# Retention into two expert layers: three tile shapes a pair in place of five, and raw weights asked for on a written schedule

## The chip, the cores and the metric

The kernel runs on one core of a Trainium2 chip. The metric is device time in microseconds (us), the median of three runs of the whole program.

## What is computed

```python
def _attn_ref(q, k, v):                       # B=4, H=8, S=576, D=64
    scores = scale * np.matmul(q, k.transpose(0, 1, 3, 2))
    gamma = 1.0 - 2.0 ** (-5.0 - np.arange(H, dtype=np.float32))
    Dmat = np.where(rel >= 0, gamma[:, None, None] ** rel[None, :, :], 0.0)
    return np.matmul(scores * Dmat[None, :, :, :], v)
def _moe_ref(x, w_gate, w_val, w_out):        # 2304 tokens, 512 wide, 1536 hidden
    g = x @ w_gate
    return (g * (1.0 / (1.0 + np.exp(-g))) * (x @ w_val)) @ w_out
def _moe2_ref(x, w_in, w_out):                # 512 wide, 2048 hidden
    r = np.maximum(x @ w_in, 0.0)
    return (r * r) @ w_out
```

A causal retention with one decay for each head, and behind it two dense layers on its output, called expert layers here. Their weights lie in DRAM as 64-bit words that hold a number's bits in another layout; the kernel turns them into 32-bit floats itself ("conversion").

## The kernel before

**Retention** works on 16 pairs of heads, four to a batch. A pair has its 576 positions in blocks of 128, the last one 64 wide. For pair `n` (loop in line 571) TensorE makes the scores inside each block (`scores`, line 453: two heads, 64 rows by 128 columns of the array each), DVE multiplies them by the mask into `p_sb`, or `pl` for the last block, and TensorE makes `sums` of k and v for each block (in `states`, line 472), from which ACT (a copy) and DVE (two steps) build the states `sb` that are carried from block to block. The outputs of a pair come later: `apply` (line 507) multiplies the carried states with the scaled queries `qs` (64 by 64 tiles) and then the masked scores with v (128 by 64), and ACT copies the result into `xy` (`put`). `old` is the pair whose outputs are made while pair `n` has its scores and sums: the one before for the first pairs, then two before (`LAG`). So TensorE's order in a pair is: scores, outputs of the old pair's four blocks, scores of the last block, output of the old pair's last block, sums.

**Buffers.** The scores of four blocks have two PSUM buffers, those of the last block one. The last output and the sums share a bank (`kv`). qk tiles and k tiles have three buffers, v five. One order is kept on each engine during retention: the `Chained` wrappers (line 100) issue each instruction behind the last one of its engine.

**Loads** are all issued by SP, in program order: the qk, k and v tiles of pair `n + 2` (576, 256 and 320 KB), then raw weights of 512 KB if there is a place (`prefetch`, line 130). There are two buffers in `raw_p` and one, `raw3`, that goes round in `spare`. The raw weight with index `n - LOADS_FROM` is allowed from pair `n` = 3 on; a load into a buffer that is still being converted holds SP until it is free, with all that stands behind it.

**Conversion** (`words`, line 158) takes two ACT and four DVE instructions a weight, given out in five units by `pump`: up to 25 units, five weights, during retention, from pair 5 on four a pair. DVE and ACT also build the first operands (`wi`, `wb`) and, from pairs 10 and 14 on, the differences of tokens (`xy`) and their split into a high and a low part (`xo_h`, `xo_l`, `xs`), one pair of tiles for each of seven operands (`renew`, line 297).

**Expert stages** follow: seven products of Strassen's kind for each system of weights, given out by slots (line 815), each of three matmuls for the high and low parts. Their order is no longer chained; the scheduler sets it.

Of the kernel before, what the change touches and what calls it, by code (L numbers as in the profile page):

```python
# [9 lines left out]
F32 = mybir.dt.float32  # L10
F32R = mybir.dt.float32r
U16 = mybir.dt.uint16
U32 = mybir.dt.uint32
AF = mybir.ActivationFunctionType
ALU = mybir.AluOpType
PSUM = bass.MemoryType.PSUM

B, H, S, D = 4, 8, 576, 64
# [3 lines left out]
P = 128  # L22
# [3 lines left out]
NC = -(-S // P)  # L26
N = 512
M0 = 256
M1 = 512
# [14 lines left out]
WARM = 5  # L44
UNITS_EARLY = 5
HOLD = 5
LOADS_FROM = 3

PACE = {(1, 0): (10, 1.6, 0.3), (1, 1): (8, 2.0, 0.0), (2, 0): (2, 0.0, 1.0)}

# [3 lines left out]
STATE = (0, 1, 3, 5)  # L54
# [7 lines left out]
def retention_moe_kernel(  # L62
# [13 lines left out]
    def pool(stack, name, bufs, **kw):  # L76
        return stack.enter_context(
            tc.tile_pool(name=name, bufs=bufs, reuse_waits="tile", **kw)
        )
# [10 lines left out]
    ps_g = pool(ctx, "ps_g", 1, space=PSUM)  # L90
# [33 lines left out]
    order = [(1, what, f) for k in range(F1 // 2) for what in "gvo" for f in (2 * k, 2 * k + 1)]  # L124
    order += [(2, what, f) for k in range(F2 // 2) for what in "io" for f in (2 * k, 2 * k + 1)]
    raw_t, w_t = {}, {}
    spare, ready = [], {}
    loads = {"next": 0, "raw": 0, "open": False, "cap": len(order) - 1, "held": 0, "turn": 0}

    def prefetch(upto):  # L130

        while loads["next"] <= min(upto, len(order) - 1):
            i = loads["next"]
            if loads["raw"] < 2:
                loads["raw"] += 1
                flat, back = raw_p.tile([P, 1024], U32, tag="raw", name="raw"), False
            elif spare:
                flat, back = spare.pop(0), True
            else:
                return  # L140
            loads["next"] += 1
            ph, what, f = order[i]
            src = (w1, w2)[ph - 1][f, :, ("gvo", "io")[ph - 1].index(what), :].bitcast(U32)
            sp.dma_start(out=flat.rearrange("p (a n) -> p a n", a=2), in_=src.rearrange("p (a n) -> p a n", a=2))
            raw_t[i] = flat, back
# [41 lines left out]
    def conversion():  # L187
        for i, key in enumerate(order):
            while loads["held"] > HOLD - 1:
                yield "held"  # L190
            prefetch(max(i, min(i + 4, loads["cap"])))
            flat, back = raw_t[i]
            for n, wt in enumerate(words(flat)):
                if n == 2:
                    finish(i - 1)
                else:
                    yield
            del raw_t[i]
            if not back:
                loads["raw"] -= 1  # L200
            elif loads["open"]:
                spare.append(flat)
            if key[0] == 1:
                ready[key] = wt.bitcast(F32)
                loads["held"] += 1
            else:
                w_t[i] = wt
            yield
        finish(len(order) - 1)
        yield  # L210
# [38 lines left out]
    def pump(k=1):  # L249
        for _ in range(k):  # L250
            if pumped["n"] < pumped["limit"]:
                pumped["n"] += next(convert, None) != "held"
# [127 lines left out]
    xo_p = pool(ctx, "xo_p", 1, side="right")  # L380

    with ExitStack() as st:
# [6 lines left out]
        sb_p = pool(st, "sb_p", 3)  # L389
        ps_s = pool(st, "ps_s", 1, space=PSUM)  # L390

        qk_t, k_t, v_t, q_t, p_t, sb_t = ({} for _ in range(6))
        rs = [slice(h * D, (h + 1) * D) for h in range(2)]
        pairs = [(b, hp) for b in range(B) for hp in range(NP)]
# [50 lines left out]
        def width(c):  # L445
            return min(P, S - c * P)
# [6 lines left out]
        def scores(n, cs):  # L453

            w, nx, hp = width(cs[0]), len(cs), pairs[n][1]
            ps = ps_s.tile([P, 2, 512], F32, tag=f"s{nx}", name="s", bufs=1 + (nx > 1))
            for x, c in enumerate(cs):
                at = slice(c * P, c * P + w)
                for h, r in enumerate(rs):
                    pe.matmul(  # L460
                        ps[:w, h, x * w:(x + 1) * w], qk_t[n][r, 1, at], qk_t[n][r, 0, at],
                        start=True, stop=True, skip_group_check=True,
                    )
            pt = p_p.tile([P, 2, nx, w], F32, tag="p", name="p_sb") if nx > 1 else p_last[n % 3]
            dve.tensor_tensor(
                out=pt[:w], in0=ps[:w, :, :nx * w].rearrange("p h (c q) -> p h c q", c=nx),
                in1=mask_sb[:w, hp, :, None, :w].to_broadcast([w, 2, nx, w]), op=ALU.mult,
            )
            for x, c in enumerate(cs):
                p_t[n, c] = pt[:, :, x, :]  # L470

        def states(new, old):


            bank = ps_g.tile([P, 512], F32, tag="v", name="kv")
            if old is not None:
                apply(old, True, bank[:, 256:256 + D])
            if new is None:
                put(old, True, bank[:, 256:256 + D])
                return  # L480
            kt, vt = k_t[new], v_t[new]
            ps = bank[:, :256].rearrange("p (c d) -> p c d", d=D)
            for c in range(NC - 1):
                for r in rs:
                    pe.matmul(
                        ps[r, c], kt[:, c, r], vt[:, c, r], start=True, stop=True,
                        skip_group_check=True,
                    )
            if old is not None:
                put(old, True, bank[:, 256:256 + D])  # L490
            sb_t[new] = sb = sb_p.tile([P, 6, D], F32, tag="sb", name="sb")
            hp = pairs[new][1]
            act.copy(sb[:, 0:6:2], ps[:, :3])
            for scalar, at, before, sums in (
                (qs_sb[:, hp, -1:], slice(1, 6, 2), sb[:, 0:6:2], ps[:, 1:]),
                (decay2[:, hp], slice(3, 6, 2), sb[:, :2], sb[:, 3:6:2]),
            ):
                dve.scalar_tensor_tensor(
                    out=sb[:, at], in0=before, scalar=scalar, in1=sums, op0=ALU.mult, op1=ALU.add,
                )  # L500

        def put(n, last, bank):
            b, hp = pairs[n]
            t0 = b * S + last * (NC - 1) * P
            act.copy(xy[:, hp, t0:t0 + bank.shape[-1]], bank)

        def apply(n, last, bank):

            cs = (NC - 1,) if last else range(NC - 1)

            def dst(c):
                return bank if last else bank[:, c * P:(c + 1) * P]

            for c in (cs if last else range(1, NC - 1)):
                at = slice((c - 1) * P, (c - 1) * P + width(c))
                for r in rs:
                    pe.matmul(
                        dst(c)[r], sb_t[n][r, STATE[c - 1]], q_t[n][r, at],
                        start=(c in (1, NC - 1)), stop=False, skip_group_check=True,
                    )  # L520
            for c in cs:
                pt = p_t.pop((n, c))
                for h, r in enumerate(rs):
                    pe.matmul(
                        dst(c)[r], v_t[n][:, c, r], pt[:, h, :],
                        start=False, stop=True, skip_group_check=True,
                    )

# [38 lines left out]
        last = len(pairs) - 1  # L567
        pumped["limit"] = 5 * UNITS_EARLY
        loads["open"] = True
        spare.append(raw2_p.tile([P, 1024], U32, tag="raw", name="raw3"))  # L570
        for n in range(last + 1 + LAG):
            new, nxt = n <= last, n + 1 <= last
            old = n - 1 if 1 <= n <= SOON else n - LAG if n > SOON + 1 else None
            if n + 2 <= last:
                load_qk(n + 2)
                load_kv(n + 2)
            if n >= LOADS_FROM:
                loads["cap"] = n - LOADS_FROM
                prefetch(loads["cap"])
            if new:  # L580
                scores(n, range(NC - 1))
            fill = int(n > LOADS_FROM + 1)
            pump(2 * fill)
            if old is not None:
                bank_o = ps_g.tile([P, 512], F32, tag="g", name="o")
                apply(old, False, bank_o)
                put(old, False, bank_o)
            if new:
                scores(n, (NC - 1,))
            if new or old is not None:  # L590
                states(n if new else None, old)
            if nxt:
                prep_state(n + 1)
            begin(n, 1)
            pump(fill)
            begin(n, 0)
            if n == 0:
                warm(1)
            pump(fill)
            if n % 2:  # L600
                begin(n, 1)
            else:
                catch_up()
# [180 lines left out]
    for n, (ph, p, k, what) in enumerate(systems):  # L784
        if what == "v":
            for x, which in enumerate("acb" if p == 0 else "ab"):
                at = n + 3 if which == "b" and n < flip - 1 else n + 2
# [27 lines left out]
    for n in range(end + 4):  # L815
        ph, p, k, what = systems[n] if n < end else (0, None, 0, "")
# [119 lines left out]
```

## Time and profile before

| | us |
|---|---|
| median of three runs | 875.05 (874.41 to 877.57) |
| profiled execution, span from the first to the last instruction | 875.1 |
| TensorE busy (PE) | 863.9, 99% |
| DVE busy | 642.8, 73% |
| ACT busy | 400.9, 46% |
| POOL busy | 122.2, 14% |

The profile is of one execution; its span and the median differ by less than 0.1 us. Matmuls overlap, so TensorE's busy time only says where it has nothing at all. "Releaser" is the instruction or transfer whose end let a waiting engine go on. A retention matmul in 32-bit floats stands as two instructions in the trace and as one in the program's order.

### The profile page before, as it was taken

The page shows a single profiled execution, that of the slowest core. Times are in us where ns is not written, and L with a number is a line of the kernel's source. Part 1 is how long each engine was busy: PE and PEld are TensorE (multiplying, and loading weights), DVE is VectorE, ACT ScalarE, POOL GpSimd, SP SyncE. Part 2 cuts the span into 40 slices and gives each one's busy share as a digit, 9 for nine tenths or more (in the row PEclk, how much of TensorE's full clock was granted, in tenths as well). Part 3 has the DMA queues.
Part 4 walks back from the last instruction along what each step waited for, and adds up shares of the span by engine and source line. Part 5 has one row for each costly group of instructions (what it writes and reads, how often), then busy time and mean ns, then how long its engine had stood idle before and what let it go on. Part 6 is the DMA issues. An engine that isn't in the chain of part 4 may idle for free.

```text
span 875.1 us, 13516 instructions
## 1 busy us (share of the span) xinstructions
PE 863.9 (99%) x5064; PEld 746.0 (85%) x5064; DVE 642.8 (73%) x1002; ACT 400.9 (46%) x709; POOL 122.2 (14%) x135
## 2 busy tenths in 40 slices
PE   9989999999999999999999999999999999999998
PEld 7878888888888888888888899989899988998987
DVE  3899999998976899677647999999534467533544
ACT  3657777565544544644325466554233233232310
POOL 3343343223130010000002311120000000000000
PEclk9999999999999999999999999999999999999999
DMA  9994777755554489878745388988666465656412
GB/s 337 402 356 160 253 249 249 264 186 211 196 192 154 139 282 379 297 273 288 253 141 185 144 315 328 361 304 313 206 239 215 126 226 210 190 202 204 164 41 73
DMA packets 75218, 203.62 MB, mean 233 GB/s; under 512 B 7696, under 2 KB 18448, under 8 KB 75152
## 3 DMA queue, kind: packets, MB, share of 16 engines
q1 hardware_dynamic: 74720, 202.34, 65.8%
q8 instruction: 40, 0.66, 0.3%
q10 hardware_dynamic: 432, 0.41, 0.1%
q14 instruction: 26, 0.21, 0.1%
HBM read 138.23 MB, written 64.49 MB: 232 GB/s over the span
## 4 chain that ended last, share of the span: by engine, by line
PE 86%; DVE 7%; DMA 4%; issue 2%; ACT 1%; SPq 0%; POOL 0%; DVEq 0%; POOLq 0%; ACTq 0%
PE oacc L113 42%; PE g L113 24%; PE v L113 12%; PE z L113 6%; DVE w L113 3%; DMA qk_sb<-in_qk 3%; DVE wi L113 1%; PE o L113 1%; DMA k_sb<-in_kv 1%; DMA qs_sb<-in_qscale 1%; PE s L113 1%; DVE xy L113 1%; DVE cbg L113 0%; PE kv L113 0%; DVE xo_l L113 0%
## 5 line engine op out<-in xcount | busy, mean ns | idle before, releaser
L113 PE MATMUL g<-xo_h,wi 128*128 128x384 f32 (+1 forms) x768 | 238.3, 364 | 0.0
L113 PE MATMUL oacc<-wo,ho_hi 128*128 128x512 f32 (+1 forms) x584 | 179.5, 388 | 0.0
L113 PEld LDWEIGHTS g<-xo_h,wi 128*128 128x128 f32 x768 | 142.5, 188 | 17.1
L113 PE MATMUL oacc<-ho_hi,wo 128*128 128x512 f32 (+1 forms) x480 | 151.1, 370 | 0.5 <-ACT xy L113 0.5
L113 DVE TENSOR_TENSOR xy<-oacc,xy 128x512 f32<-128x512 f32 (+1 forms) x155 | 99.6, 648 | 59.6 <-PE oacc L113 59.1
L113 PE MATMUL g<-xo_l,wi 128*128 128x384 f32 (+1 forms) x384 | 139.6, 364 | 0.0
L113 PEld LDWEIGHTS oacc<-wo,ho_hi 128*128 128x128 f32 x584 | 108.4, 188 | 19.2
L113 PE MATMUL v<-xo_h,wi 128*128 128x512 f32 (+1 forms) x384 | 123.2, 364 | 0.0
L113 PE MATMUL oacc<-wo,ho_lo 128*128 128x512 f32 (+1 forms) x292 | 113.3, 390 | 0.0
L113 PEld LDWEIGHTS oacc<-ho_hi,wo 128*128 128x128 f32 x480 | 88.1, 188 | 17.6 <-ACT xy L113 1.3
L113 PE MATMUL oacc<-ho_lo,wo 128*128 128x512 f32 (+1 forms) x240 | 89.1, 371 | 0.0
L113 PEld LDWEIGHTS g<-xo_l,wi 128*128 128x128 f32 x384 | 72.1, 188 | 8.4
L113 DVE TENSOR_SCALAR w<-w 128x512 f32<-128x512 f32 (+1 forms) x136 | 64.9, 480 | 18.0 <-ACT w L113 17.0
L113 PEld LDWEIGHTS v<-xo_h,wi 128*128 128x128 f32 x384 | 71.2, 188 | 8.0
L113 DVE TENSOR_TENSOR cbg<-v,cbg 128x384 f32<-128x384 f32 (+1 forms) x72 | 43.1, 598 | 45.8 <-ACT cbg L113 24.3
L113 ACT ACTIVATE cag<-g 128x384 f32<-128x384 f32 (+1 forms) x36 | 19.0, 528 | 125.2 <-PE g L113 125.1
L113 PE MATMUL v<-xo_l,wi 128*128 128x512 f32 (+1 forms) x192 | 69.8, 363 | 0.0
L113 PEld LDWEIGHTS oacc<-wo,ho_lo 128*128 128x128 f32 x292 | 54.8, 188 | 11.2
L113 PE MATMUL z<-xo_h,wi 128*128 128x512 f32 (+1 forms) x192 | 62.5, 365 | 0.0
L113 ACT CAST ho_hi<-cbg 128x768 fp32r<-128x768 f32 (+1 forms) x36 | 32.7, 908 | 45.5 <-DVE cbg L113 44.4
L113 DVE SCALAR_TENSOR_TENSOR w<-raw,w 128x512 uint32<-128x512 uint32 x68 | 52.5, 773 | 0.7
L113 PEld LDWEIGHTS oacc<-ho_lo,wo 128*128 128x128 f32 x240 | 45.1, 188 | 8.7
(90 smaller groups left out, 1295.6 us busy)
## 6 DMA issues: line engine op xcount, KB each, us to landing
wi<-win SPq DMA_DIRECT2D x84, 512.0 KB, 4.2
raw<-in_w SPq DMA_DIRECT2D x68, 512.0 KB, 4.9
win<-wi SPq DMA_DIRECT2D x60, 512.0 KB, 3.6
wo<-wsp SPq DMA_DIRECT2D x44, 512.0 KB, 6.4
wsp<-wo SPq DMA_DIRECT2D x28, 512.0 KB, 5.2
qk_sb<-in_qk SPq DMA_DIRECT2D x15, 576.0 KB, 7.4
wst<-w SPq DMA_DIRECT2D x32, 256.0 KB, 6.0
wi<-win SPq DMA_DIRECT2D x28, 256.0 KB, 5.4
```

Of the source, the lines that this page charges most:

```text
L113: i = op(*args, **kw)
```

## The change

Three things. In retention the scores of the last block now come directly behind those of the others, the old pair's outputs make all products with carried states first (`carried`) and all products inside a block behind them (`inside`), the last block's output included, and the sums follow. So a pair has the shapes 64x128, 64x64 and 128x64 once each. Raw weights are allowed at the pairs of a table (`RAW_AT`: index 0 from pair 1, 1 from pair 3, 2 from pair 4, then 6, 7, 13, 13 and 14), and two more buffers take one raw weight each: the high and the low tile of operand 3 of the first expert pass, which are idle until then. Conversion starts with pair 4 in place of 5, with three units in even pairs and four in odd ones.

```diff
-LOADS_FROM = 3
+RAW_AT = (1, 3, 4, 6, 7, 13, 13, 14)
+CONVERT_FROM = 4
...
             if loads["raw"] < 2:
                 loads["raw"] += 1
                 flat, back = raw_p.tile([P, 1024], U32, tag="raw", name="raw"), False
+            elif once:
+                flat, back = once.pop(0), None
             elif spare:
                 flat, back = spare.pop(0), True
...
-        def states(new, old):
-            bank = ps_g.tile([P, 512], F32, tag="v", name="kv")
-            if old is not None:
-                apply(old, True, bank[:, 256:256 + D])
...
+        def sums(n, bank):
...
+        def states(n, bank):
...
+        def carried(n, cs, bank):
+            for c in cs:
                 at = slice((c - 1) * P, (c - 1) * P + width(c))
                 for r in rs:
                     pe.matmul(
-                        dst(c)[r], sb_t[n][r, STATE[c - 1]], q_t[n][r, at],
+                        dst(c, bank)[r], sb_t[n][r, STATE[c - 1]], q_t[n][r, at],
                         start=(c in (1, NC - 1)), stop=False, skip_group_check=True,
                     )
+
+        def inside(n, cs, bank):
             for c in cs:
                 pt = p_t.pop((n, c))
...
+        for x in "hl":
+            once.append(xo_p.tile([P, 2, M1], U32, tag=f"x{x}3", name="raw5").rearrange("p a n -> p (a n)"))
...
-            if n >= LOADS_FROM:
-                loads["cap"] = n - LOADS_FROM
-                prefetch(loads["cap"])
+            loads["cap"] = sum(x <= n for x in RAW_AT) - 1
+            prefetch(loads["cap"])
             if new:
                 scores(n, range(NC - 1))
-            fill = int(n > LOADS_FROM + 1)
-            pump(2 * fill)
+            fill = int(n >= CONVERT_FROM)
+            pump(fill * (1 + n % 2))
+            if new:
+                scores(n, (NC - 1,))
+            bank_v = ps_g.tile([P, 512], F32, tag="v", name="kv")
+            bank_l = bank_v[:, 256:256 + D]
             if old is not None:
                 bank_o = ps_g.tile([P, 512], F32, tag="g", name="o")
-                apply(old, False, bank_o)
+                carried(old, range(1, NC - 1), bank_o)
+                carried(old, (NC - 1,), bank_l)
+                inside(old, range(NC - 1), bank_o)
+                inside(old, (NC - 1,), bank_l)
                 put(old, False, bank_o)
             if new:
-                scores(n, (NC - 1,))
-            if new or old is not None:
-                states(n if new else None, old)
+                sums(n, bank_v)
+            if old is not None:
+                put(old, True, bank_l)
+            if new:
+                states(n, bank_v)
```

On TensorE, one pair in the middle of retention (`s` scores, `o` and `kv<-qs`, `kv<-pl` outputs of the old pair, `kv<-v_sb,k_sb` sums). Before:

```order
13 L113 MATMUL s<-qk_sb 128x128 x8
14 L113 MATMUL o<-qs,sb 64x128 x6
15 L113 MATMUL o<-p_sb,v_sb 64x128 x8
16 L113 MATMUL s<-qk_sb 64x64 x2
17 L113 MATMUL kv<-qs,sb 64x64 x2
18 L113 MATMUL kv<-pl,v_sb 64x64 x2
19 L113 MATMUL kv<-v_sb,k_sb 64x64 x8
```

and now:

```order
13 L114 MATMUL s<-qk_sb 128x128 x8
14 L114 MATMUL s<-qk_sb 64x64 x2
15 L114 MATMUL o<-qs,sb 64x128 x6
16 L114 MATMUL kv<-qs,sb 64x64 x2
17 L114 MATMUL o<-p_sb,v_sb 64x128 x8
18 L114 MATMUL kv<-pl,v_sb 64x64 x2
19 L114 MATMUL kv<-v_sb,k_sb 64x64 x8
```

The two 64x64 rows have moved: the last scores ahead of the outputs, the last carried product ahead of the products with v.

On SP, the loads from pair 4 on (each `qk_sb` row opens a pair; `raw` rows are raw weights). Before, from pair 5:

```order
23 L113 DMA qk_sb<-in_qk 128x1152
24 L113 DMA k_sb<-in_kv 128x512
25 L113 DMA v_sb<-in_kv 128x640
26 L113 DMA raw<-in_w 128x1024
27 L113 DMA qk_sb<-in_qk 128x1152
28 L113 DMA k_sb<-in_kv 128x512
29 L113 DMA v_sb<-in_kv 128x640
30 L113 DMA raw<-in_w 128x1024
```

and now, from behind pair 3 to the second raw weight:

```order
20 L114 DMA raw<-in_w 128x1024
21 L114 DMA qk_sb<-in_qk 128x1152
22 L114 DMA k_sb<-in_kv 128x512
23 L114 DMA v_sb<-in_kv 128x640
24 L114 DMA qk_sb<-in_qk 128x1152
25 L114 DMA k_sb<-in_kv 128x512
26 L114 DMA v_sb<-in_kv 128x640
27 L114 DMA raw<-in_w 128x1024
```

The raw weights stood behind pairs 5, 6, 7, 8, 9, 10, 12 and 14 and stand behind pairs 3, 5, 6, 8, 9 and, three of them, 15.

On DVE, from pair 4's masked product to pair 6's (`w` rows are steps of a conversion). Before:

```order
19 L113 TENSOR_TENSOR p_sb<-s,mask_sb 128x1024
20 L113 TENSOR_TENSOR pl<-s,mask_sb 64x128
21 L113 SCALAR_TENSOR_TENSOR sb<-sb,qs_sb,kv 128x3x64
22 L113 SCALAR_TENSOR_TENSOR sb<-sb,decay_245 128x2x64
23 L113 TENSOR_TENSOR p_sb<-s,mask_sb 128x1024
24 L113 TENSOR_SCALAR w<-w 128x512
25 L113 TENSOR_TENSOR pl<-s,mask_sb 64x128
```

and now:

```order
19 L114 TENSOR_TENSOR p_sb<-s,mask_sb 128x1024
20 L114 TENSOR_TENSOR pl<-s,mask_sb 64x128
21 L114 SCALAR_TENSOR_TENSOR sb<-sb,qs_sb,kv 128x3x64
22 L114 SCALAR_TENSOR_TENSOR sb<-sb,decay_245 128x2x64
23 L114 TENSOR_SCALAR w<-w 128x512 x2
24 L114 TENSOR_TENSOR p_sb<-s,mask_sb 128x1024
25 L114 SCALAR_TENSOR_TENSOR w<-raw,w 128x512
26 L114 ISA w<-raw,w 128x1024
27 L114 TENSOR_TENSOR pl<-s,mask_sb 64x128
```

The first two DVE steps of the first weight come ahead of pair 5's product, the other two directly behind it. From pair 10's `p_sb` to the end of retention DVE's order is the same in both. In the first expert steps the scheduler has moved some instructions past each other; there the split of operand 3, which was the second of three, stands 15 places later, behind the conversion of the weight that was loaded into its tile.

## Rows read from the trace of the kernel before

**Rows 1.** The page, part 4: shares of the chain that ended last, by engine.

```profile
PE 86%; DVE 7%; DMA 4%; issue 2%; ACT 1%; SPq 0%; POOL 0%; DVEq 0%; POOLq 0%; ACTq 0%
```

**Rows 2.** TensorE's waits after 79.08 us (total, times, longest); timelines of PE, DVE.

```profile
PE oacc L113 <- ACT xy L113: 0.9, 3, 0.4
...
79.08 0.50 PE L113 MATMUL g<-xo_h,wi 128*128 128x512 f32 x1
...
93.62 0.68 DVE L113 TENSOR_TENSOR wi<-w,wi 128x512 fp32r<-128x512 f32 x1
...
100.75 0.39 PE L113 MATMUL v<-xo_h,wi 128*128 128x512 f32 x1
```

**Rows 3.** Stretches: length, busy PE, PEld, DVE, ACT, POOL (instructions), clock, DMA share, GB/s.

```profile
30.00:40.00 10.00, 9.51 (x170) 7.93 (x171) 7.98 (x16) 6.64 (x16) 3.54 (x5) 1.00 1.03 401
25.14:49.74 24.60, 23.19 (x416) 19.29 (x412) 20.71 (x41) 17.41 (x42) 9.00 (x13) 1.00 0.97 368
49.74:73.83 24.09, 20.54 (x356) 17.21 (x358) 22.99 (x34) 13.77 (x30) 11.38 (x12) 1.00 0.88 341
```

**Rows 4.** Timeline of TensorE: start, length, instruction, [idle before <- releaser]; pairs 7, 10, 11.

```profile
32.44 1.16 PE L113 MATMUL s<-qk_sb 64*128 64x128 f32 x16 [0.37 <-DMA qk_sb<-in_qk]
...
44.99 1.16 PE L113 MATMUL s<-qk_sb 64*128 64x128 f32 x16
...
51.28 1.16 PE L113 MATMUL s<-qk_sb 64*128 64x128 f32 x16 [2.20 <-DMA qk_sb<-in_qk]
```

**Rows 5.** Timeline of SP's queue around the sixth raw weight.

```profile
44.41 0.33 SPq L113 DMA_DIRECT2D raw<-in_w  x1
44.84 0.99 SPq L113 DMA_DIRECT2D qk_sb<-in_qk  x1
```

**Rows 6.** Timeline of DVE: masked products of pairs 10, 11 and 15, and others.

```profile
39.96 0.69 DVE L113 TENSOR_TENSOR wi<-w,wi 128x512 fp32r<-128x512 f32 x1
...
49.74 1.22 DVE L113 TENSOR_TENSOR p_sb<-s,mask_sb 128x1024 f32<-128x1024 f32 x1
...
53.88 1.23 DVE L113 TENSOR_TENSOR xo_l<-xy,xo_h 128x1024 fp32r<-128x1024 f32 x1 [0.89 <-ACT xo_h L113]
...
56.43 1.21 DVE L113 TENSOR_TENSOR p_sb<-s,mask_sb 128x1024 f32<-128x1024 f32 x1
...
60.20 1.36 DVE L113 TENSOR_TENSOR wi<-w,wi 128x512 fp32r<-128x512 f32 x1
...
73.83 1.22 DVE L113 TENSOR_TENSOR p_sb<-s,mask_sb 128x1024 f32<-128x1024 f32 x1
```

**Rows 7.** Timeline of TensorE: a pair without waits, and the end of retention.

```profile
13.70 1.16 PE L113 MATMUL s<-qk_sb 64*128 64x128 f32 x16
...
15.59 1.09 PE L113 MATMUL o<-p_sb,v_sb 128*64 128x128 f32 x16
16.61 0.27 PE L113 MATMUL s<-qk_sb 64*64 64x64 f32 x2
...
16.99 0.34 PE L113 MATMUL kv<-pl,v_sb 128*64 128x64 f32 x4
17.15 0.64 PE L113 MATMUL kv<-v_sb,k_sb 128*64 128x64 f32 x16
17.72 1.16 PE L113 MATMUL s<-qk_sb 64*128 64x128 f32 x16
...
75.88 0.33 PE L113 MATMUL kv<-qs,sb 64*64 64x64 f32 x4
76.14 0.34 PE L113 MATMUL kv<-pl,v_sb 128*64 128x64 f32 x4
```

**Rows 8.** DVE's groups by shape, 20 to 80 us: busy, mean ns, idle before.

```profile
L113 DVE TENSOR_SCALAR w<-w 128x512 f32<-128x512 f32 x5 | 2.3, 466 | 2.8 <-ACT w L113 2.8
```

**Rows 9.** Timeline of ACT: the k tile of pair 11.

```profile
52.00 0.91 ACT L113 ACTIVATE k_sb<-k_sb,ks_sb 128x256 f32<-128x256 f32 x2 [2.44 <-DMA k_sb<-in_kv]
```

**Rows 10.** Timeline of POOL: the query scaling of pair 13.

```profile
59.32 1.69 POOL L113 TENSOR_TENSOR qs<-qk_sb,qs_sb 128x384 f32<-128x384 f32 x1 [2.63 <-PE kv L113]
```

More of the change, by code (lines that the diff above doesn't have):

```diff
@@ L126, in retention_moe_kernel @@
     raw_t, w_t = {}, {}
-    spare, ready = [], {}
+    spare, once, ready = [], [], {}
     loads = {"next": 0, "raw": 0, "open": False, "cap": len(order) - 1, "held": 0, "turn": 0}
@@ L198, in conversion @@
             del raw_t[i]
-            if not back:
+            if back is False:
                 loads["raw"] -= 1
-            elif loads["open"]:
+            elif back and loads["open"]:
                 spare.append(flat)
@@ L470, in scores @@
                 p_t[n, c] = pt[:, :, x, :]
-        def states(new, old):
-            bank = ps_g.tile([P, 512], F32, tag="v", name="kv")
-            if old is not None:
-                apply(old, True, bank[:, 256:256 + D])
[L478 to L481, printed above, removed]
+        def sums(n, bank):
+            kt, vt = k_t[n], v_t[n]
             ps = bank[:, :256].rearrange("p (c d) -> p c d", d=D)
@@ L488, in states @@
                     )
[L489 to L492, printed above, removed]
+        def states(n, bank):
+            ps = bank[:, :256].rearrange("p (c d) -> p c d", d=D)
+            hp = pairs[n][1]
+            sb_t[n] = sb = sb_p.tile([P, 6, D], F32, tag="sb", name="sb")
             act.copy(sb[:, 0:6:2], ps[:, :3])
-            for scalar, at, before, sums in (
+            for scalar, at, before, more in (
                 (qs_sb[:, hp, -1:], slice(1, 6, 2), sb[:, 0:6:2], ps[:, 1:]),
@@ L498, in states @@
                 dve.scalar_tensor_tensor(
-                    out=sb[:, at], in0=before, scalar=scalar, in1=sums, op0=ALU.mult, op1=ALU.add,
+                    out=sb[:, at], in0=before, scalar=scalar, in1=more, op0=ALU.mult, op1=ALU.add,
                 )
@@ L505, in put, with dst @@
             act.copy(xy[:, hp, t0:t0 + bank.shape[-1]], bank)
[L507 to L514, printed above, removed]
+        def dst(c, bank):
+            return bank if c == NC - 1 else bank[:, c * P:(c + 1) * P]
+        def carried(n, cs, bank):
+            for c in cs:
                 at = slice((c - 1) * P, (c - 1) * P + width(c))
@@ L524, in apply @@
                     pe.matmul(
-                        dst(c)[r], v_t[n][:, c, r], pt[:, h, :],
+                        dst(c, bank)[r], v_t[n][:, c, r], pt[:, h, :],
                         start=False, stop=True, skip_group_check=True,
```

## The prediction

> **What bounds the kernel now.** I read the page first, then stretches of the span, then the engines' order of time. The chain that ended last gives TensorE 86%, DVE 7% and DMA 4% [rows 1]; what is to be found is where the 11% of the latter two lie. From 79.08 us on, TensorE runs the expert stages, and after that point it waits three times, 0.9 us in all, each time for ACT [rows 2]. What the change can win lies therefore before 79.08, in the retention stage; a microsecond gained there reaches the end unless the 0.9 us grows.
>
> Inside retention the limit changes hands. Between 30 and 40 us the 16 DMA engines are full (share 1.03) while DVE has 8.0 of 10 us; between 49.74 and 73.83 DVE has 22.99 of 24.09 us and TensorE 20.54 [rows 3]. TensorE's clock is granted whole (1.00) in all of them. The scores show the first regime: pair 7 waits 0.37 us for its qk tile, pair 10 starts at 44.99 at the end of the same queue, and pair 11 starts at 51.28 after 2.20 us without data [rows 4]. That last wait has its cause on SP's queue: the sixth raw weight (index 5) was issued only at 44.41, because the buffer it takes was still being converted, and the qk of pair 11 stands behind it, issued at 44.84 [rows 5]. The masked product p_sb shows the second regime. DVE begins it for pair 10 at 49.74, 4.75 us after that pair's scores, for pair 11 at 56.43 and for pair 15 at 73.83 [rows 6]: there DVE lags TensorE by about a pair, and DVE's order is fixed.
>
> **The change, part by part.** *Tile changes.* A pair without waits takes 17.72 - 13.70 = 4.02 us and crosses five borders between tile shapes [rows 7]. Price of one, lower end: four small matmuls need 17.15 - 16.99 = 0.16 us with no border behind them, and 76.14 - 75.88 = 0.26 us for four with one, so 0.10 us. Upper end: the 0.27 us that a small matmul takes from start to end [rows 7]. Two borders fewer make a pair 3.5 to 3.8 us long; I take 3.75, by the pair of rows that is nearest to a border alone. The matmuls at 16.61 start 0.07 us before the group of 15.59 has its modelled end (16.68), so no full emptying is seen there. The Trainium skill (TensorEngine Tiling (Array Packing), Key Properties) says that a change of tiling mode drains TensorE; by that rule the price would be near the upper end and the pair near 3.5 us, the sum below would stay, and the first rival would come out at 866.6.
>
> What do 0.2 to 0.5 us a pair buy? In pairs 1 to 3 TensorE comes some 0.8 us earlier to the qk tiles, and from pair 6 on it waits for them. After pair 10 it waits for DVE. So I cost this part at nothing as long as DMA and DVE cover it, except in the two groups of outputs at the end, where two borders each go: 0.4 us. If the cover is gone it is worth the whole (first rival).
>
> *Raw weights in DMA order.* Up to pair 10's qk the bytes are the same: five raw weights ahead of it before and after. But the first now stands behind pair 3, the second behind pair 5 and the third behind pair 6, so the qk of pairs 4 to 7 have one more ahead of them. 512 KB at the 401 GB/s of 30 to 40 us [rows 3] are 1.3 us. In pair 4 what TensorE gained meets most of it; pairs 6 and 7 come 1.3 us later (pair 7 at 33.7, not 32.44); pairs 8 to 10 come at the old times, pair 10 no earlier than 45.0. From pair 11 on no raw weight stands ahead until all pairs are asked for; one pair is 1152 KB, 2.9 us, less than a pair of TensorE. The wait of 2.20 us goes. The fifth raw weight still waits on SP for the conversion of the second, as before, with the qk of pair 10 behind it.
>
> *Conversion from pair 4.* The same 25 units are done, but from pair 4 and at 3 or 4 units a pair in place of 4 from pair 5. Today DVE has 20.71 us of work in the 24.60 us from pair 5's p_sb to pair 10's, 3.9 us idle [rows 3], of which the first step of a conversion, waiting for ACT's part of a weight, has 2.8 [rows 8]. With the raw data there a pair sooner that idling can go; the 1.3 us that pairs 6 and 7 come later, and 0.5 us behind later sums, are idle time of a new kind. So p_sb of pair 10 starts some 2.0 us earlier, at 47.7, which is 2.7 us behind its scores and so allowed. Bounds: nothing, and 3.6 us (scores at 45.0 plus the 1.1 us that they run).
>
> *Pairs 10 to 15.* The order on DVE from pair 10 on is that of before. At 53.88 it had waited 0.89 us for ACT's xo_h [rows 6], and ACT had waited 2.44 us for the k tile of pair 11 until 52.00 [rows 9], which stands behind the held raw weight on SP too. Without that, xo_l starts at about 51.3 and pair 11's p_sb moves by 2.6 to 3.4 us, say 3.0. From 56.43 to 73.83 are 17.4 us of DVE work with next to no gap. Some of it is stretched: the 128x512 subtraction at 60.20 took 1.36 us, its like at 39.96 0.69 us, and a POOL product runs from 59.32 to 61.01 [rows 6, 10]. I count two such stretches, 1.3 us in all; whether they stay depends on where POOL's products fall, so 0.5 us comes back, between 0 and 1.3. The Trainium skill (SBUF — State Buffer, section SBUF: two separate sides) says that such a DVE instruction and one of POOL exclude each other on a shared port; by that rule nothing comes back while POOL has its product in every pair, and the forecast would be 872.0. The row agrees in kind: the subtraction ends 0.55 us after the product.
>
> *A wait that is added.* The last block's scores now stand ahead of all outputs of the old pair. They have one PSUM buffer, so they wait for DVE's pl of the pair before, and the outputs, the sums, ACT's copy and DVE's sb queue behind that wait. Chain: 0.25 us for those scores, 2.1 for the outputs, 0.6 for the sums, 0.5 on ACT, about 3.4 us; DVE in that time has sb 0.7, its other work, p_sb 1.1 and pl 0.2. Only with less than 1.4 us of other work does it wait, which holds behind pair 13 (one split of 1.1 us): 0.3 us, within the rounding.
>
> *Operand tiles lent.* The weight with index 7 sits in the low tile of operand 3 until it is converted in the first expert steps, so DVE's split of operand 3 moves 15 places back. The instruction that stands there today starts at 93.62, and TensorE first reads operand 3 at 100.75 [rows 2]: some 6 us of cover behind a split of 1.1 us, so nothing.
>
> **Sum.** DVE at pair 15: 3.0 + 0.5 = 3.5 us earlier. TensorE begins the expert stages 3.5 + 0.4 = 3.9 us earlier, but its 0.9 us of waits there are set by ACT and DVE, which gained 3.5, so they become 1.3. Net 3.5 us. The profiled execution has a span of 875.1 us and the median of the runs is 875.05, so both give the same: **871.5 us**. Ends of this case: 2.0 us (nothing back after pair 10) and 4.8 us (3.4 + 1.3 and rounding), 873.0 and 870.2.
>
> **The rivals.** *TensorE becomes the bound* (22 in 100). If DVE's idle time and stretches all close, six pairs of 3.75 us follow 45.0, then two groups of outputs, 4.6 us: the expert stages start at 72.1, 7.0 us earlier, 868.1 us. For it: the idle DVE time before pair 10; against it: 22.99 us of unchanged work from pair 10 to pair 15 [rows 3].
>
> *The stage only changes its excuse* (20 in 100). Pairs 6 and 7 late by 1.3 us throw back DVE's state steps as well, which wait for sums and ACT, and p_sb of pair 10 stays near 49; the later pairs are DVE work of the same length. Gain 0.5 to 1.5 us, 874.0. For it: the stage follows DMA up to 45 us whatever TensorE does.
>
> *Slower* (7 in 100). The added wait closes a loop: last scores behind pl, outputs and sums behind them, sb behind the sums, the next pl behind sb. If ACT, with its puts, k scalings and operand casts in one order, brings the state copy 1 us later than reckoned, DVE idles some 1.2 us in each of pairs 11 to 15: 6 us lost against 3.5 gained, 877.5 us. It decides once ACT's copy ends over 1.5 us behind the sums.
>
> **How the numbers follow.** Forecast 51, first rival 22, second 20, third 7 in 100. A measurement of this kernel tells about 0.5%, 4.4 us, from no change. Faster by more: the first rival and the upper quarter of the forecast, 0.36. Slower by more: the far half of the third rival, 0.04. Within: 0.60. The range reaches from the first rival's time to the middle of the second's and leaves out half of the first, the third and the second's end: 868.1 to 874.8.
>
> **What would show it.** Right: scores of pair 7 near 33.7 us and of pair 10 near 45; no gap before pair 11; p_sb of pair 10 near 47.7 and of pair 15 near 70.3; the first expert product near 75.2; waits of 0.9 to 1.5 us behind it. The tile step is right if a pair without waits takes 3.5 to 3.8 us. Wrong: scores of pair 10 well before 44, since DMA then was not the limit; idle TensorE before the last scores in pair after pair; or a gap at the first product that reads operand 3.

## The result: slower, and where the profile after shows the time

The change takes **880.37 us** (median of 6 runs, 879.66 to 882.14) against 875.01 for the kernel before (6 runs, 874.41 to 877.57): ratio 1.0057, 95% interval 1.0043 to 1.0071. Forecast were 871.5 and a range from 868.1 to 874.8. The profiled execution of the change has a span of 878.4 us and a time of 880.17; in all runs the time is 1.8 us more than the span. So the profile of before, whose span was 875.1, belongs to an execution of about 876.9 us, not to the median. A run of the same instructions that took 875.0 us was profiled later (e7, span 873.2); it is the better partner, and **what is compared below is the change with e7**.

The chain of the change gives TensorE, DVE and DMA what it gave them before [rows 1], so the shares tell nothing. TensorE's list of waits up to 200 us (without its last line, 0.2 us) does:

```profile
PE s L114 <- DVE pl L114: 6.3, 6, 1.9
PE s L114 <- DMA qk_sb<-in_qk: 3.2, 4, 1.2
PE kv L114 <- DMA v_sb<-in_kv: 1.3, 2, 1.2
PE g L114 <- DVE one L114: 1.2, 1, 1.2
PE o L114 <- ACT xy L114: 0.9, 2, 0.7
PE oacc L114 <- ACT xy L114: 0.6, 1, 0.6
PE oacc L114 <- DVE xy L114: 0.5, 2, 0.3
PE g L114 <- ACT cbg L114: 0.3, 1, 0.3
```

The first line is the wait that the prediction priced at 0.3 us, now once in each of pairs 9 to 14; in e7 it is 0.7 us, once. The last three lie in the expert stages, 1.4 us where before had 0.9 [rows 2].

Timeline of TensorE in the change (start, length, instruction, [idle before <- releaser]): scores of pairs 4, 5, 7, 8, 10, 11 and 14, last scores of pair 14, its sums, scores of pair 15, the last group of outputs, first expert product.

```profile
22.81 1.42 PE L114 MATMUL s<-qk_sb 64*128 64x128 f32 x20 [1.13 <-DMA qk_sb<-in_qk]
...
26.40 1.37 PE L114 MATMUL s<-qk_sb 64*128 64x128 f32 x18 [1.24 <-DMA qk_sb<-in_qk]
...
34.83 1.37 PE L114 MATMUL s<-qk_sb 64*128 64x128 f32 x18 [0.42 <-DMA qk_sb<-in_qk]
...
38.55 1.16 PE L114 MATMUL s<-qk_sb 64*128 64x128 f32 x16
...
46.50 1.16 PE L114 MATMUL s<-qk_sb 64*128 64x128 f32 x16
...
51.01 1.16 PE L114 MATMUL s<-qk_sb 64*128 64x128 f32 x16
...
65.64 1.16 PE L114 MATMUL s<-qk_sb 64*128 64x128 f32 x16
68.69 0.33 PE L114 MATMUL s<-qk_sb 64*64 64x64 f32 x4 [1.89 <-DVE pl L114]
...
70.76 0.64 PE L114 MATMUL kv<-v_sb,k_sb 128*64 128x64 f32 x16
71.33 1.36 PE L114 MATMUL s<-qk_sb 64*128 64x128 f32 x18
...
78.33 0.87 PE L114 MATMUL o<-qs,sb 64*64 64x128 f32 x12 [0.66 <-ACT xy L114]
...
80.38 0.51 PE L114 MATMUL g<-xo_h,wi 128*128 128x512 f32 x1
```

The same places in e7 (pair 11, then pairs 14 and 15):

```profile
49.90 1.16 PE L113 MATMUL s<-qk_sb 64*128 64x128 f32 x16 [0.51 <-DMA qk_sb<-in_qk]
...
66.69 0.33 PE L113 MATMUL s<-qk_sb 64*64 64x64 f32 x4 [0.71 <-DVE pl L113]
...
67.53 0.64 PE L113 MATMUL kv<-v_sb,k_sb 128*64 128x64 f32 x16
68.10 1.16 PE L113 MATMUL s<-qk_sb 64*128 64x128 f32 x16
...
77.15 0.50 PE L113 MATMUL g<-xo_h,wi 128*128 128x512 f32 x1
```

A pair with nothing to wait for takes 38.55 - 34.83 = 3.72 us where it took 4.02 [rows 7]: the two borders are saved, at 0.15 us each. But from the scores of pair 15 to the first expert product are 9.05 us in both (80.38 - 71.33, 77.15 - 68.10): there waits for ACT's copies of the outputs (0.66 us, the longest) give the borders back. And the scores of pair 15 come 3.23 us later: 2.00 us because the last scores of pair 14 start later (68.69 against 66.69), and 1.23 because 2.64 us stand between these two places where 1.41 stood. Three numbers divide the loss. Timeline of DVE in the change: masked products of pairs 10, 11 and 15, and steps before and between them.

```profile
46.59 0.82 DVE L114 TENSOR_SCALAR w<-w 128x512 uint32<-128x512 uint32 x1
...
50.09 1.24 DVE L114 TENSOR_TENSOR wi<-s,wi 128x256 fp32r<-128x256 f32 x1
51.26 1.21 DVE L114 TENSOR_TENSOR p_sb<-s,mask_sb 128x1024 f32<-128x1024 f32 x1
...
55.09 1.49 DVE L114 SCALAR_TENSOR_TENSOR w<-raw,w 128x512 uint32<-128x512 uint32 x1
56.50 1.21 DVE L114 TENSOR_TENSOR p_sb<-s,mask_sb 128x1024 f32<-128x1024 f32 x1
...
74.10 1.22 DVE L114 TENSOR_TENSOR p_sb<-s,mask_sb 128x1024 f32<-128x1024 f32 x1
```

And of DVE in e7, pairs 10, 11 and 15, and the step ahead of pair 11's:

```profile
50.05 1.22 DVE L113 TENSOR_TENSOR p_sb<-s,mask_sb 128x1024 f32<-128x1024 f32 x1
...
53.89 0.69 DVE L113 SCALAR_TENSOR_TENSOR w<-raw,w 128x512 uint32<-128x512 uint32 x1
54.49 1.22 DVE L113 TENSOR_TENSOR p_sb<-s,mask_sb 128x1024 f32<-128x1024 f32 x1
...
71.90 1.22 DVE L113 TENSOR_TENSOR p_sb<-s,mask_sb 128x1024 f32<-128x1024 f32 x1
```

| stretch | e7 | change | lost |
|---|---|---|---|
| start to masked scores of pair 15 | 71.90 | 74.10 | 2.20 |
| from there to the first expert product | 5.25 | 6.28 | 1.03 |
| from there to the end of the span | 796.05 | 798.02 | 1.97 |
| span | 873.2 | 878.4 | 5.2 |

The 2.20 us are there early: p_sb of pair 10 is 1.21 us late and that of pair 11 2.01, of which 0.80 is the one step at 55.09 (1.49 us, in e7 0.69). The 1.97 us come soon too: 300 matmuls behind the first expert product TensorE is 1.88 us later than in e7 (59.09 and 57.21 us after that product).

### The profile page after: what moved, and what is told of

Read it like the earlier page. It is cut to its first block, busy times and chain, and to the rows that moved or that the text cites. A ratio compares the mean times of both kernels' runs of the same rounds, so it can differ in the third digit from the quotient of the medians.

```text
span 878.4 us, 13505 instructions
## 1 busy us (share of the span) xinstructions
PE 860.4 (98%) x5064; PEld 747.1 (85%) x5064; DVE 644.5 (73%) x1002; ACT 399.6 (45%) x709; POOL 125.8 (14%) x135
## 4 chain that ended last, share of the span: by engine, by line
PE 85%; DVE 7%; DMA 4%; ACT 2%; issue 2%; POOL 0%; SPq 0%; ACTq 0%; DVEq 0%; POOLq 0%
PE oacc L114 41%; PE g L114 25%; PE v L114 12%; PE z L114 6%; DVE w L114 3%; DMA qk_sb<-in_qk 2%; PE o L114 1%; DVE wi L114 1%; DMA k_sb<-in_kv 1%; DMA mask_sb<-in_mask 1%; DVE p_sb L114 1%; PE s L114 0%; DVE ho_lo L114 0%; DVE cbg L114 0%; DVE xy L114 0%
## 5 line engine op out<-in xcount | busy, mean ns | idle before, releaser
L114 DVE TENSOR_SCALAR w<-w 128x512 f32<-128x512 f32 (+1 forms) x136 | 67.8, 501 | 17.3 <-ACT w L114 16.5
L114 ACT COPY cbg<-g 128x384 f32<-128x384 f32 (+1 forms) x72 | 37.0, 513 | 31.8 <-PE g L114 29.4
```

The lines of the kernel that those rows point to most:

```text
L114: i = op(*args, **kw)
```

## The experiments

All times are medians in us, with the kernel before run beside them on the same chip (875.46 for e0 to e3, 875.2 for e4 to e10, 875.08 for e11 and e12). Theory W, with which the tests began: the added wait for DVE is what the change pays for.

**The kernel before again** (e0, e7), no edit in the order of its work.

> The kernel before, unchanged, for a second profile. Both theories: the first expert product at 78.5 to 79.6 us, scores of pair 5 at 23.3 to 24.3 and of pair 10 at 44.5 to 45.5, p_sb of pair 10 at 49.2 to 50.2. If these scatter by more than 1 us, the difference of 1.3 us between the first expert products of before (79.08) and of the change (80.38) is not to be read from one profile of each.

> The kernel before, instruction for instruction, written with the functions of the change. Its runs lie at 874.5 to 876 and, one in four, at 877 to 878; the two profiles so far are of 876.4 and 876.9. A profile of a run near 875 would show where 1.5 to 2 us lie: by the theory that the loads of the first pairs jitter, first expert product at 77 to 78 and 796.0 from there on; by the theory that the expert stages jitter, 79 and 794.5.

They took 876.4 and 875.0. The first expert product came at 78.50 and 77.15, and 796.1 us followed in each, as in the first profile (79.08, then 796.0). So in these three it is retention that differs from run to run. The 2.20 us without data before pair 11 [rows 4] were 0.51 us in e7; of the nine profiles here with the loads of before, one other (e1) has 1.95 us there, and the other seven at most 0.61.

**One half of the change at a time** (e1, e2).

e1 is the change with the loads and the pump of before, e2 the kernel before with those of the change. e1 against the change (e2 against before is its mirror image, with the lent tiles):

```diff
-RAW_AT = (1, 3, 4, 6, 7, 13, 13, 14)
-CONVERT_FROM = 4
+LOADS_FROM = 3
...
-            loads["cap"] = sum(x <= n for x in RAW_AT) - 1
-            prefetch(loads["cap"])
+            if n >= LOADS_FROM:
+                loads["cap"] = n - LOADS_FROM
+                prefetch(loads["cap"])
...
-            fill = int(n >= CONVERT_FROM)
-            pump(fill * (1 + n % 2))
+            fill = int(n > LOADS_FROM + 1)
+            pump(2 * fill)
```

> TensorE's order of the change (last scores ahead of the old pair's outputs), raw loads and conversion as before. Theory W (the added wait: last scores wait for DVE's pl with 2.6 us of outputs and sums queued behind, where before 1.8 us of outputs ran during that wait): TensorE waits for pl 4 us or more in all, the stage's end is 1 to 2.5 us later than before, 876.5 to 878.5 us. Theory L (the raw loads asked for sooner push the qk tiles of pairs 4 to 10 back by 1.5 to 2.6 us, and everything late comes from there): this kernel is at 872 to 875 us, its pair without waits takes 3.7 us, scores of pair 5 at or ahead of 23.8 us.

> Raw loads and conversion of the change, TensorE's order as before. Theory W: the loads are harmless or good, 873 to 875.5 us, first expert product at 78 to 79.2. Theory L: scores of pair 5 at about 26 us, p_sb of pair 10 at 51 or later, the first expert product at 80 to 81, 877.5 to 880 us.

Measured: the order alone 879.12 (8 runs, ratio 1.0034, 1.0021 to 1.0048), the loads alone 876.80 (12 runs, 1.0011, 1.0003 to 1.0020). Some 3.7 and 1.3 us against 5.4 for both: each half is slower by itself, and the medians nearly add up. Both times lie outside what theory W had said (876.5 to 878.5, and 873 to 875.5). Up to p_sb of pair 10 the halves do not add up: 50.15 in e1, 49.63 in e2, 50.05 in e7, but 51.26 in the change.

**pl sooner on DVE** (e3): DVE's product for the last scores directly behind p_sb, ahead of the conversion steps.

```diff
-            pump(fill * (1 + n % 2))
             if new:
                 scores(n, (NC - 1,))
+            pump(fill * (1 + n % 2))
```

> The change, with DVE's masking of the last block (pl) directly behind the four blocks' (p_sb), ahead of the conversion steps of that place. Theory W: TensorE's waits for pl fall from 6.3 us to under 4.5 and the time from 880.4 to 877.5 to 879.5. Theory L: waits may fall, the time stays at 880 to 881, because DVE's work after pair 10 is the same and starts as late.

880.45 (6 runs, 1.0046, 1.0031 to 1.0061), and TensorE still waits 5.0 us for pl. So pl ahead of the conversion steps gains nothing; that it cannot is not shown, since all six runs list a mean granted clock of TensorE below 1.00 (0.994 to 0.998), and the profiled one, the slowest, has 0.50 from 25 to 31 us.

**The order in the last pairs, or in all others** (e4, e5), loads as before: e1 with a switch, in whose first branch stands TensorE's order of the change and in the other that of before. e4's is shown; e5 has `n < 14`.

```diff
+            if n > 13:
...
+            else:
+                if old is not None:
...
+                    inside(old, range(NC - 1), bank_o)
+                    put(old, False, bank_o)
+                if new:
+                    scores(n, (NC - 1,))
...
```

> Loads as before; the three-change order of TensorE only from pair 14 on (pairs 14 and 15 and the two rounds that drain outputs), the order of before until pair 13. Theory T (the order costs at the end of retention: behind DVE's last product for the last scores stand 2.6 us of TensorE work where 1.4 stood): first expert product 6.3 us after the last masked scores product (before 5.25), and 876.5 to 879.5 us, most of what the order alone cost (879.1 against 875.5). Theory S (it costs in the early and middle pairs, by waits of the last scores for DVE): the 6.3 us show too but are taken back, and the time is 875.0 to 876.2.

> Loads as before; the three-change order of TensorE only in pairs 0 to 13, the order of before in pairs 14 and 15 and the rounds that drain. Theory T: first expert product 5.25 us after the last masked scores product, and 875.0 to 876.2 us, since nothing that TensorE wins or loses in the middle pairs reaches DVE. Theory S: 876.5 to 879.5 us, with waits for DVE's last-scores product of some 3 us in TensorE's list of waits.

e4 took 877.82 (10 runs, 1.0026, 1.0015 to 1.0037), e5 875.71 (10 runs, 1.0011, 0.9998 to 1.0024). Theory T holds: the last two pairs and the two rounds behind them, which only make outputs, hold most of what the order costs (2.6 of some 3.7 us); what the other pairs cost is not clear of noise. TensorE in e4, last scores of pair 14, outputs and scores of pair 15; then 1 us stretches with TensorE's busy time, granted clock, DMA share and GB/s:

```profile
66.82 0.37 PE L113 MATMUL s<-qk_sb 64*64 64x64 f32 x2 [2.54 <-DVE pl L113]
...
68.71 1.82 PE L113 MATMUL o<-p_sb,v_sb 128*64 128x128 f32 x16
...
71.04 1.37 PE L113 MATMUL s<-qk_sb 64*128 64x128 f32 x18
...
73.16 1.09 PE L113 MATMUL o<-p_sb,v_sb 128*64 128x128 f32 x16
```

```profile
66.00:67.00 1.00, 0.18 (x5) 0.92 1.03 405
67.00:68.00 1.00, 1.00 (x14) 0.50 1.05 425
68.00:69.00 1.00, 1.00 (x14) 0.50 1.04 424
69.00:70.00 1.00, 1.00 (x12) 0.50 0.57 223
```

In e7 TensorE does the outputs, then waits, and 68.10 - 66.69 = 1.41 us after the wait the scores of pair 15 begin. With the last scores ahead of the outputs it waits first, and 71.33 - 68.69 = 2.64 us follow. DVE's pl comes at the same place of DVE's order either way, so the difference, 1.2 us, is lost. In the change 1.03 of it are the second row of the table; the rest, 0.2, lies in the first (from p_sb of pair 14 to that of pair 15 are 3.69 us, in e7 3.50). In this execution of e4 the longer wait cost more: after 2.54 us of standing TensorE's clock was granted at 0.50 (1.2 of 2.4 GHz) for some 3 us, and the same 16 matmuls took 1.82 us, not 1.09. The profile of the change itself shows 1.00 throughout, so its 5.2 us hold no part of this. The medians may: seven of e4's ten runs, four of e1's eight and four of the change's six list a mean clock of 0.996 to 0.998, and all twelve of e2's 1.00. The runs of e1 and e4 at 1.00 have medians of 878.25 and 877.23, so up to about 0.9 and 0.6 us of these two costs may be the clock; in the change the two runs at 1.00 (880.14 and 880.17) lie 0.2 us below its median.

**The change with the old tail** (e8): e5's switch in the change.

> The change with one part undone: pairs 14 and 15 and the two rounds that drain have TensorE's order of before. Theory T (the end of retention carries the order's cost, the loads carry the rest by themselves): first expert product 5.25 us after the last masked scores product (6.28 in the change), first expert product at 77.5 to 79, 797.1 us from there as with the loads alone, and 876.5 to 878 us. Rival (the loads and the order lose together in pairs 5 to 10, where the change's masked scores product of pair 10 comes at 51.26 against 50.05): 879 to 880.5 us.

877.56 (9 runs, 1.0027, 1.0018 to 1.0037), 2.8 us less than the change. From p_sb of pair 15 to the first expert product it has 5.25 us again, and 797.24 from there on. Its rival is right in one thing: p_sb of pair 10 still comes at 51.06, so the early order and the sooner loads together lose there what neither loses alone.

**Last scores at the end of a pair** (e9; e10 with the change's order in pairs 0 to 11): from pair 12 on the last scores follow the sums.

```diff
+            if n > 11:
...
+                    carried(old, range(1, NC - 1), bank_o)
+                    carried(old, (NC - 1,), bank_l)
+                    inside(old, range(NC - 1), bank_o)
+                    inside(old, (NC - 1,), bank_l)
...
+                    sums(n, bank_v)
+                    scores(n, (NC - 1,))
```

> The kernel before, but from pair 12 on the last scores stand behind the sums, at the end of a pair, and the carried parts of both outputs stand together: four tile changes, and all of TensorE's work of the pair lies ahead of the wait for DVE. If that wait is what the order pays for, its 0.7 us goes and two borders per pair go: first expert product about 1 us sooner than before (76.2 where 77.15 was), and 874.0 to 874.8 us. If DVE's own line sets the end of retention, first expert product as before or the expert stages longer by what was won, and 875.0 to 875.8 us. Slower than 876: the scores of the next pair now stand behind the wait and reach DVE late.

> Loads as before; three-change order in pairs 0 to 11, and from pair 12 on the last scores at the end of a pair. As the run with the last scores last, with what the three-change order won or lost in the middle: its run without the tail had 875.7 us median and its profile 872.9 us of span. Expected 874.0 to 875.3 us if the middle is free, 875.5 to 876.5 if the waits for DVE there cost.

875.93 (10 runs, 1.0013, 1.0001 to 1.0025) and 877.50 (8 runs, 1.0023, 1.0010 to 1.0036): no gain, and e10 is 1.0 us above the highest time that was expected, for a reason not looked for. The wait for pl is gone from e9, and another stands in its place, before the carried part of the last output:

```profile
66.53 0.33 PE L113 MATMUL kv<-qs,sb 64*64 64x64 f32 x4 [1.58 <-DVE sb L113]
```

That output lies in the bank of the sums, so whoever writes it early waits until DVE's sb has read the sums of the pair before. In e9 this wait ends 0.16 us sooner than the one for pl in e7 (66.53, 66.69), but 11.08 us follow to the first expert product (77.61) where 10.46 did: again the work behind the wait decides.

**No tile lent** (e6): e2 without the two operand tiles.

```diff
-        for x in "hl":
-            once.append(xo_p.tile([P, 2, M1], U32, tag=f"x{x}3", name="raw5").rearrange("p a n -> p (a n)"))
```

> TensorE's order as before; raw weights at the pairs of the change and conversion from pair 4, but no operand tile lent: the third weight's load waits for a freed buffer. Theory L (the lent tiles make the expert stages longer, since an operand tile comes free only when the eighth weight is converted): time from the first expert product to the end 796.0 to 796.3 us as before (797.1 with the loads alone), first expert product at 77.5 to 78.5, and 874.5 to 875.8 us. Theory R (any other hour of the conversions makes the scheduler of the build set the expert stages in another order, whatever is lent): 797 us or more from the first expert product on, and 876 to 878 us.

876.36 (10 runs, one of them 4866 us; 1.0010, 1.0000 to 1.0020), with 796.82 us from the first expert product on. Theory R, nearly (it said 797 or more): by these two profiles the lent tiles are at most a quarter of e2's microsecond. The build's scheduler sets TensorE's order in the expert stages. It came out the same in before and in all kernels with the loads of before (e1, e4, e5, e9, e10, but for three rows at most), and these have 796.0 to 796.4 us there; e6 has an order of its own; e2 and e8 share another order, 797.07 and 797.24; the change and e3 a third, 798.02 both, though e3 enters it 2.5 us later.

**POOL's products away** (e11, e12): from pair 4 on ACT scales the queries, by one factor per partition, so the outputs' values are others.

```diff
+            if n >= 4:
+                act.mul(qs, qk_t[n][:, 0, P:], qs_sb[:, hp, -1:])
-            for c, m in ((0, 3 * P), (3 * P, D)):
+            for c, m in ((0, 3 * P), (3 * P, D)) if n < 4 else ():
```

> The kernel before, but from pair 4 on the scaled queries are made by one ACT multiplication with one factor per partition instead of POOL's two products (another factor, so the values of the outputs change; the work of all other engines stays). Theory P (DVE's conversion steps take up to twice as long where a POOL product runs beside them): the 1.23 us of SCALAR_TENSOR_TENSOR w, the 1.35 of wi and the 1.77 of xy fall to 0.69, 0.69 and 1.22, last masked scores product at 70 to 71 (71.90 in the profile of a usual run), time 873 to 874.5 us. Rival (they are slow for a reason of their own): same durations, 875 us or more.

> The change with the same replacement of POOL's products (values of the outputs change). Theory P: wi<-s,wi 0.4 us (1.24 in the change, 0.42 before), TENSOR_SCALAR w 0.4 each, and the masked scores product of pair 10 within 0.5 us of the other kernel's; the change costs less over its partner than 5.3 us, about 4, since the part that lies in stretched steps (some 1 to 2 us) goes, while the end of retention (1 us) and the expert stages (2 us) stay: 876.5 to 878.5 us. Rival: the distance stays 5.3 us.

875.24 (10 runs, 0.9994, 0.9985 to 1.0003) and 878.70 (7 runs, 1.0035, 1.0023 to 1.0047): the distance falls from 5.4 to 3.5 us. Some 0.6 us of that is e11's own, whose expert stages take 796.64 us in the order of before; the rest lies in retention. e11 by itself gains nothing, though 873 to 874.5 us were expected: its steps are shorter, but p_sb of pair 15 comes only 0.45 us sooner than e7's. DVE's busy time from 19 us to p_sb of pair 15 (stretch, length, busy PE, PEld, DVE, ACT, POOL with instructions, clock, DMA share, GB/s), in e7:

```profile
19.00:71.90 52.90, 49.62 (x880) 41.63 (x878) 46.54 (x82) 34.09 (x80) 23.58 (x32) 1.00 0.96 372
```

in the loads alone (e2), the change and e12:

```profile
19.00:72.28 53.28, 49.76 (x880) 41.78 (x878) 48.44 (x81) 33.93 (x80) 24.85 (x32) 1.00 0.99 369
```

```profile
19.00:74.10 55.10, 45.44 (x862) 41.55 (x862) 49.44 (x81) 33.68 (x80) 26.13 (x32) 1.00 0.97 363
```

```profile
19.00:72.29 53.29, 45.13 (x858) 41.26 (x854) 45.04 (x81) 40.07 (x91) 5.16 (x8) 1.00 0.97 358
```

The same instructions of DVE (the 82nd only touches the end) cost 46.5, 48.4 and 49.4 us, and 45.0 without POOL's products; before without them (e11) has 45.5. So DVE does stand still less with the loads sooner, 52.90 - 46.54 = 6.4 us in e7 and 53.28 - 48.44 = 4.8 in e2 (5.7 in the change), and what it wins it pays in longer steps. From p_sb of pair 5 to that of pair 10, in e7 and in the change:

```profile
25.19:50.05 24.86, 23.39 (x418) 19.50 (x416) 20.59 (x40) 17.73 (x43) 9.14 (x14) 1.00 0.98 374
```

```profile
27.86:51.26 23.40, 21.41 (x415) 19.71 (x413) 21.07 (x39) 15.78 (x40) 11.71 (x16) 1.00 1.03 400
```

Its idle time there falls from 4.27 to 2.33 us, but the stretch begins 2.67 us later. POOL in the change beside the rows of DVE above, and those steps in e12, with one that waits:

```profile
46.26 1.30 POOL L114 TENSOR_TENSOR qs<-qk_sb,qs_sb 128x384 f32<-128x384 f32 x2 [2.49 <-DMA qk_sb<-in_qk]
...
49.59 1.93 POOL L114 TENSOR_TENSOR qs<-qk_sb,qs_sb 128x384 f32<-128x384 f32 x2
...
54.24 2.52 POOL L114 TENSOR_TENSOR qs<-qk_sb,qs_sb 128x384 f32<-128x384 f32 x2 [2.04 <-PE kv L114]
```

```profile
49.84 0.42 DVE L114 TENSOR_TENSOR wi<-s,wi 128x256 fp32r<-128x256 f32 x1
50.17 1.22 DVE L114 TENSOR_TENSOR p_sb<-s,mask_sb 128x1024 f32<-128x1024 f32 x1
...
54.17 1.23 DVE L114 TENSOR_TENSOR xo_l<-xy,xo_h 128x1024 fp32r<-128x1024 f32 x1 [1.15 <-ACT xo_h L114]
55.31 0.68 DVE L114 SCALAR_TENSOR_TENSOR w<-raw,w 128x512 uint32<-128x512 uint32 x1
```

1.24 and 1.49 us have become 0.42 and 0.68, and p_sb of pair 10 comes 0.64 us before e11's (50.81), where in the change it came 1.21 after e7's.

No kernel here beats the one before.

## Why the prediction was wrong, step by step

- **The sum's base failed.** "So both give the same" set a span of 875.1 beside a median of 875.05. The execution was one 1.9 us longer than the usual, and the wait of 2.20 us before pair 11, on which the largest term stood (3.0 us in pairs 10 to 15), is 0.51 us in a usual one (e7). The change does remove it (51.01 has no wait); there was little to remove. From p_sb of pair 10 to that of pair 11 e7 takes 4.44 us where the first profile took 6.69, and the change 5.24.
- **"Tile changes" was right:** 3.72 us where 3.75 was taken. It was also right that DMA, then DVE cover it; the 0.4 us at the end did not come, since ACT's copies are waited for instead. By the Trainium skill (TensorEngine Tiling (Array Packing), Key Properties) a change of tiling mode drains TensorE; the 0.15 us that a border cost lie nearer to the prediction's lower end, 0.10 us, than to the 0.27 us that it put by that rule.
- **"Raw weights in DMA order" was right in kind.** It said that TensorE's gain would meet most of the extra load in pair 4, and that pairs 8 to 10 would come at the old times. Waits for data of 1.13 and 1.24 us stand in pairs 4 and 5 instead; pair 7's scores came at 34.83 (33.7 forecast) and pair 10's at 46.50 (45.0).
- **"Conversion from pair 4" was mis-sized.** p_sb of pair 10 was forecast at 47.7; it came at 51.26, and at 49.63 with the loads alone. DVE's idle time ahead of it did fall by 1.9 us, about as reckoned; but p_sb of pair 5, from which this was counted, came 2.67 us late behind those waits, and DVE's 39 steps from there took 21.07 us where 40 had taken 20.59.
- **The stretches were counted the wrong way.** The working let 0.5 us come back; in the whole stretch DVE's steps became 2.9 us longer than in e7, and without POOL's products some 1.4 us of the loss at p_sb of pair 15 go (below). The prediction counted the stretches that were there and did not reckon that more steps can come to lie under POOL's products. The Trainium skill (SBUF — State Buffer, SBUF: two separate sides) says that an instruction of DVE with two inputs in SBUF and one of POOL that reads SBUF exclude each other. The rows agree in kind: without the product the subtraction is back at 0.42 us. By that rule alone nothing would have come back.
- **"A wait that is added" failed.** It asked when pl comes, and took 0.3 us. Its sign of being wrong, TensorE idle before the last scores in pair after pair, came six times, 6.3 us in all; of those ahead of pair 14 e5 shows no cost clear of noise. For the one in pair 14 it should have asked how much work lies behind the wait: 2.64 us in place of 1.41. The third rival named a loop through the added wait, some 1.2 us in each of pairs 11 to 15, and 877.5 us. The wait was the right one, but no loop closes: the 1.2 us are lost once, by the scores of pair 15 and all of TensorE's work behind them.
- **"Operand tiles lent" at nothing** stands within what was measured. What no term held is that the expert stages come out in another order and longer, by 1.0 us (e2) to 2.0 us (the change).

Of the table: of the first 2.20 us, e12 against e11 leaves 0.84 (72.29 against 71.45), so about 1.4 go with POOL's products; the next 1.03 are the order at the end of retention, gone in e8; the 1.97 go with the order of the expert stages. Of the 0.84 us, 0.2 are again the order at the end; the rest arises from p_sb of pair 10, where e12 is still 0.64 us ahead, to that of pair 11, 5.74 us in e12 and 4.47 in e11: DVE in e12 waits there 1.15 us for ACT's xo_h, and in e11 it does not. These are differences of single profiles, and p_sb of pair 15 alone lies between 71.90 and 73.83 us in the three profiles of before, so the parts are estimates. That the order itself, and not the time at which DVE and ACT enter, makes those 1.97 us was not tried alone: no kernel ran the retention of before with the other order. For it speaks that the change, e3 and e12, which share the order and enter it at 80.38, 82.88 and 78.39 us, all have 798.0 us there.

## What to carry to other kernels

Price a wait by the work that is queued behind it on the critical engine, not by its own length: here a short instruction moved ahead of 1.2 us of independent work cost these 1.2 us. Before a stall is counted as a gain, look whether a second profile of the same kernel has it. Where an engine is close to full, less idle time is no gain until its busy time is seen to stay.

## What the hardware showed unasked

A 128x256 subtraction of DVE took three times its time beside POOL's product (1.24 against 0.42 us), more than the factor of two in the rows of before [rows 6, 10]. The masked products, which read PSUM, kept 1.21 to 1.23 us throughout. And behind a wait of 2.54 us at the end of retention TensorE's clock was granted at 0.50 for 3 us in e4, so that this wait cost more than it lasted; the wait of 2.20 us in the first profile of before left it at 1.00 [rows 3].
